# Another order for the last five chunks of an attention-and-adapters kernel

## The chip, the core and the metric

The kernel runs on one core of one Trainium2 chip, as one program. The metric is the device time of that program in microseconds. A core has TensorE (PE in the profile; PEld is its weight load), VectorE (DVE), ScalarE (ACT), GpSimd (POOL) and SyncE (SP), which here only issues DMAs. The engines run side by side; each takes its own instructions in order and waits where it needs what another has not finished.

## What is computed

Two stages follow each other. The first is attention with a pooled key and value: q is 4 x 12288 x 128, and kv, 4 x 384 x 32 x 128, is averaged over 4 x 4 patches into 768 keys of each batch.

```
kv_flat = kv_pool.reshape(B, -1, C) @ w_sr      # keys and values are the same rows
s = q @ kv_flat.T / sqrt(C);  a = softmax(s);  x = a @ kv_flat
```

The second is a mixture of eight small adapters on the 49152 rows x. The two largest of eight logits choose two adapters, and a softmax over those two gives their weights.

```
logits = x @ w_gate;  w = softmax(the two largest logits)
out = x + sum over the two of  w * ((x @ A[e]) @ B[e])      # A: 128x16, B: 16x128
```

## The kernel before, in words

The 49152 rows are handled as 96 **chunks** of 512 rows (T), each as 4 slices (S) of 128 rows, 24 chunks to a batch. K is the number of the last chunk, 95. For one chunk the steps are these, by the names of the code.

- `scores` makes the products of q and keys on TensorE in three rounds of 128x1024 into the PSUM tile sg, and ScalarE writes their exponentials into em (L246).
- `attend` multiplies em by the values extended with the gate's columns and a column of ones (vx); 24 matmuls accumulate into acc. Columns 0 to 127 are the unnormalised x, the next 8 the logits, the last the softmax's sum.
- `normalize` takes the reciprocal of the sums on VectorE (L258) and multiplies all 136 columns of the four slices (L263, 128x544) into xn.
- `top` sorts the eight logits of each slice with MAX8 (L281). `route` and `gates` make the two weights: four small operations on GpSimd (L293, L298, L299), a tanh on ScalarE (L312), and two more on GpSimd (L314, L315) into gw. A softmax over two is a tanh of half their difference. The tanh is put off in the list `later`.
- `transposes` and `down` turn x and multiply it by all eight A at once into h_ps. `gate` multiplies h_ps by gw into hg on VectorE (L347).
- hg is turned as well, `up` multiplies it by all eight B into d_ps, and `finish` adds d_ps and xn on VectorE (L360) and has SP store the 256 KB of the chunk (L361).

In the loop these steps of several chunks are woven into each other: while the scores of chunk k are made, chunk k-1 is attended and earlier ones pass the adapters. The order of every instruction on each engine is that of the program's text (`keep`): no scheduler moves any of it. When the loop ends, chunk K-5 is stored; K-4 has its hg turned and copied (tts) and still needs `up`, the addition and the store; K-3 has its hg, K-2 and K-1 wait with xn or acc, and K has only its exponentials. What follows is written out by hand with small helpers, and this **tail** is all that the change touches:

- `turn_x` and `turn_h` turn x or hg into a PSUM tile; `fetch` copies that into SBUF (tt) on ScalarE (L514, 128x512); `down_into` and `up_into` are the two adapter products; `gate_part` is the gate for some of the slices (L557).
- `part` is the attention of chunk K into the tile called o95.
- `add_here` adds and stores with VectorE reading PSUM (L542, then the DMA of L543). `carry` has ScalarE copy the product out of PSUM (L547), and `add_there` has GpSimd add xn to the copy and SP store it (L551, L552).
- `bank` gives PSUM: pool ps_m has two banks, ps_a one tile of two banks, ps_s two tiles of two banks. A tile that takes over a bank waits until its previous content has been read. Dependencies are kept for whole tiles: a write into one half of a tile waits for a reader of the other half.

In the tail before, chunk K is normalised in parts: VectorE makes the eight logit columns (L582, 128x32), ScalarE multiplies the 128 columns of x slice by slice (four instructions of 128x128, L585), and both begin when `part` is complete. Chunk K's weights are made on VectorE (L589 to L608) with a tanh on ScalarE (L606). K-4, K-1 and K (in halves) are added on VectorE, K-3 and K-2 go over ScalarE and GpSimd. K's hg is turned and copied in two halves (L634), K-1's in one piece. The last instruction with work is the addition of K's second half, and its store is the last one of the program.

Of the kernel before, what the change touches and what calls it, by code (L numbers as in the profile page):

```python
# [20 lines left out]
def kernel(  # L21
# [45 lines left out]
    def mm(*a, **k):  # L67
        return keep(nc.tensor.matmul(*a, **k))  # L68
# [187 lines left out]
    def normalize(k):  # L256
        ri = rpool.tile([P, S], FP32, tag="rinv", name="rinv")
        keep(nc.vector.reciprocal(ri, acc[k][:, :, VC]))  # L258
        k0, m = first[k], k - first[k]
        if m == 0:  # L260
            xg[k0] = xpool.tile([P, GC, S, VC], FP32, tag="xn", name="xn")
        x = xg[k0][:, m]
        keep(nc.vector.tensor_tensor(x, acc[k][:, :, 0:VC],  # L263
                                     ri.unsqueeze(2).broadcast_to([P, S, VC]), op=ALU.mult))
        xn[k] = x
# [19 lines left out]
    def route(k0):  # L285
        n = size[k0] * S
        eng = nc.gpsimd if k0 > 1 else nc.vector
        lg = xg[k0].rearrange("p m s c -> p (m s) c")[:, 0:n, C:VC]
        so = srt[k0].rearrange("p m s e -> p (m s) e")[:, 0:n]

        def over(i):
            d = rpool.tile([P, GC * S, 8], FP32, tag=f"over{i}", name=f"over{i}")[:, 0:n]
            keep(eng.tensor_tensor(  # L293
                d, lg, so[:, :, i].unsqueeze(2).broadcast_to([P, n, 8]), op=ALU.subtract))
            return d

        arg, mask = over(0), over(1)
        keep(eng.tensor_tensor(arg, arg, mask, op=ALU.add))  # L298
        keep(eng.tensor_scalar(mask, mask, 0.0, None, op0=ALU.is_ge))  # L299


        def rest():
            gates(k0, n, eng, arg, mask)

        if k0 > 3:
            later.append(rest)
        else:
            rest()
# [183 lines left out]
    def bank(pool):  # L492
        if pool is ps_m:
            return mtile([P, S, P], name="tail_ps")
        if pool is ps_a:
            return ps_a.tile([P, S, 256], FP32, tag="acc", name="acc")
        return ps_s.tile([P, 2, T], FP32, tag="sg", name="sg")

    def turn_x(k, pool):
        ps = bank(pool).bitcast(BF16).rearrange("p a b -> p (a b)")[:, 0:T].rearrange("p (s c) -> p s c", s=S)  # L500
        xb = xn[k].bitcast(U16)[:, :, 1::2].bitcast(BF16)
        for s in range(S):
            mm(ps[:, s], xb[:, s, 0:C], id_bf, is_transpose=True, start=(s == 0), stop=(s == S - 1))
        xT[k] = ps

    def turn_h(k, pool):
        ps = bank(pool).bitcast(BF16).rearrange("p a b -> p (a b)")[:, 0:T].rearrange("p (s c) -> p s c", s=S)
        for s in range(S):
            mm(ps[:, s], hg[k][:, s], id_bf, is_transpose=True, start=(s == 0), stop=(s == S - 1))
        hgT[k] = ps  # L510

    def fetch(which, k):
        sb = run.tile([P, S, P], BF16, tag="tt1", name="tt1")
        keep(nc.scalar.copy(sb, which[k]))  # L514
        which[k] = sb

    def part(k, o, js):
        for s in range(S):
            for j in js:
                mm(o[:, s, 0:VE], em[k][:, j, s * P:(s + 1) * P], vx[k // NB][:, j],  # L520
                   start=(j == 0 and s % 2 == 0), stop=(j == J - 1 and s % 2 == 1))

    def wide(o):
        return o.rearrange("p a b -> p (a b)")[:, 0:T].rearrange("p (s c) -> p s c", s=S)

    def down_into(k, pool):
        hp[k] = wide(bank(pool))
        for s in range(S):
            mm(hp[k][:, s], xT[k][:, s], a_bf, start=(s == 0), stop=(s == S - 1))

    def up_into(k, o):
        dp[k] = o
        for s in range(S):
            mm(o[:, s], hgT[k][:, s], b_bf, start=(s == 0), stop=(s == S - 1))
# [5 lines left out]
    def add_here(k, lo, hi, queue):  # L540
        osb = opool.tile([P, S, C], FP32, tag="osb", name="osb")[:, 0:hi - lo]
        keep(nc.vector.tensor_tensor(osb, dp[k][:, lo:hi], xn[k][:, lo:hi, 0:C], op=ALU.add))  # L542
        keep(queue.dma_start(dest(k)[:, lo:hi], osb))  # L543

    def carry(k):
        osb = opool.tile([P, S, C], FP32, tag="osb", name="osb")
        keep(nc.scalar.copy(osb, dp[k]))  # L547
        dp[k] = osb
# [5 lines left out]
    def gate_part(k, lo, hi):  # L554
        if lo == 0:
            hg[k] = run.tile([P, S, P], BF16, tag="hg", name="hg")
        keep(nc.vector.tensor_tensor(  # L557
            hg[k][:, lo:hi].rearrange("p s (e r) -> p (s e) r", e=E),
            hp[k][:, lo:hi].rearrange("p s (e r) -> p (s e) r", e=E),
            gw[k][:, lo:hi].rearrange("p s e -> p (s e)")  # L560
            .unsqueeze(2).broadcast_to([P, (hi - lo) * E, RK]), op=ALU.mult))

    turn_x(K - 2, ps_m)
    o95 = bank(ps_s).rearrange("p a (b c) -> p (a b) c", c=256)
    part(K, o95, range(4))
    turn_h(K - 3, ps_m)
    part(K, o95, range(4, J))
    fetch(xT, K - 2)
    for rest_ in later:
        rest_()  # L570
    later.clear()
    fetch(hgT, K - 3)

    normalize(K - 1)
    top(K - 1)
    route(K - 1)

    ri = rpool.tile([P, S], FP32, tag="rinv", name="rinv")
    keep(nc.vector.reciprocal(ri, o95[:, :, VC]))
    xn[K] = xpool.tile([P, GC, S, VC], FP32, tag="xn", name="xn")[:, 0]  # L580
    lg = rpool.tile([P, S, E], FP32, tag="lg", name="lg")
    keep(nc.vector.tensor_tensor(lg, o95[:, :, C:VC], ri.unsqueeze(2).broadcast_to([P, S, E]),  # L582
                                 op=ALU.mult))
    for s in range(S):
        keep(nc.scalar.activation(xn[K][:, s, 0:C], o95[:, s, 0:C], AF.Copy, bias=0.0,  # L585
                                  scale=ri[:, s:s + 1]))
    so = rpool.tile([P, S, 8], FP32, tag="so", name="so")
    for s in range(S):
        keep(nc.vector.max(so[:, s], lg[:, s]))  # L589
    mask = rpool.tile([P, S, E], FP32, tag="mk", name="mk")  # L590
    keep(nc.vector.tensor_tensor(mask, lg, so[:, :, 1].unsqueeze(2).broadcast_to([P, S, E]),
                                 op=ALU.is_ge))
    both = rpool.tile([P, S], FP32, tag="both", name="both")
    keep(nc.vector.tensor_tensor(both, so[:, :, 0], so[:, :, 1], op=ALU.add))
    keep(nc.vector.scalar_tensor_tensor(lg, lg, 2.0, both.unsqueeze(2).broadcast_to([P, S, E]),
                                        op0=ALU.mult, op1=ALU.subtract))

    down_into(K - 2, ps_m)
    gate_part(K - 2, 0, S)
    turn_x(K - 1, ps_m)  # L600
    dd = bank(ps_s)
    up_into(K - 4, wide(dd[:, 0:1]))
    up_into(K - 3, wide(dd[:, 1:2]))
    turn_x(K, ps_a)
    th = rpool.tile([P, S, E], FP32, tag="th1", name="th1")
    keep(nc.scalar.activation(th, lg, AF.Tanh, bias=0.0, scale=0.5))  # L606
    gw[K] = gpool.tile([P, S, E], FP32, tag="gw1", name="gw1")
    keep(nc.vector.scalar_tensor_tensor(gw[K], th, 1.0, mask, op0=ALU.add, op1=ALU.mult))  # L608
    fetch(xT, K - 1)
    fetch(xT, K)  # L610
    for rest_ in later:
        rest_()
    later.clear()
    carry(K - 3)
    add_there(K - 3)
    add_here(K - 4, 0, S, nc.sync)
    down_into(K - 1, ps_m)
    gate_part(K - 1, 0, S)
    turn_h(K - 2, ps_m)
    fetch(hgT, K - 2)  # L620
    down_into(K, ps_s)
    gate_part(K, 0, 2)
    gate_part(K, 2, S)
    up_into(K - 2, bank(ps_m))
    turn_h(K - 1, ps_a)
    fetch(hgT, K - 1)
    carry(K - 2)
    add_there(K - 2)
    ps = bank(ps_m).bitcast(BF16).rearrange("p a b -> p (a b)")[:, 0:T].rearrange("p (s c) -> p s c", s=S)
    hgT[K] = run.tile([P, S, P], BF16, tag="tt1", name="tt1")  # L630
    for lo in (0, 2):
        for s in range(lo, lo + 2):
            mm(ps[:, s], hg[K][:, s], id_bf, is_transpose=True, start=(s == lo), stop=(s == lo + 1))
        keep(nc.scalar.copy(hgT[K][:, lo:lo + 2], ps[:, lo:lo + 2]))  # L634
    up_into(K - 1, wide(bank(ps_s)))
    add_here(K - 1, 0, S, nc.sync)
    dp[K] = wide(bank(ps_s))
    for lo in (0, 2):
        for s in range(lo, lo + 2):
            mm(dp[K][:, s], hgT[K][:, s], b_bf, start=(s == lo), stop=(s == lo + 1))  # L640
        add_here(K, lo, lo + 2, nc.sync if lo else nc.scalar)


# [28 lines left out]
```

## Time and profile before

| what | value |
|---|---|
| time, median of 9 runs | 409.35 us (409.04 to 409.52) |
| the profiled execution | 409.23 us |
| its span in the profile | 407.2 us, so 2.0 us lie outside of it |
| busy: PE, DVE, ACT, POOL | 93%, 80%, 72%, 42% of the span |
| stretch 384 to 388 us (in the loop): PE busy | 3.95 of 4.00 us |
| stretch 396 to 398.5 us (in the tail): PE, DVE, ACT busy | 1.28, 1.19, 1.82 of 2.50 us |
| stretch 398.5 to 403.6 us: PE, DVE, ACT busy | 2.21, 2.27, 1.72 of 5.10 us |
| last addition (L542) ends | 403.56 us |

The profile comes from one execution, and times inside it count from its start. A line of the timeline gives start, duration (both us), engine, line, operation, the tile written and the tiles read, the shapes, and in brackets how long the engine had been idle and what ended that. A matmul's records overlap: four of 128x128 start some 0.056 us apart and each lasts 0.22 us, until its result is in PSUM. Instructions on ScalarE and VectorE overlap at their ends in the same way when the next one doesn't need the one before: copies of 128x512 on ScalarE last 0.6 us and start 0.47 us apart. "Granted clock" is the share of TensorE's full clock.

### The profile page before, as it was taken

To read this page: it belongs to the slowest core of one execution; us is meant where nothing else is said; L and a number is where in the kernel's file an instruction comes from. 1 tells how busy PE (TensorE), PEld (TensorE's weight loads), DVE (VectorE), ACT (ScalarE), POOL (GpSimd) and SP (SyncE) were. 2 spreads that over 40 slices of the span, in tenths; PEclk is the share of its full clock that TensorE was granted. 3 is DMA by queue.
4 is the path that set the end of the run, shared out by engine and by line. 5 is a ranking of instruction groups with operands and counts; after the bars stand their busy time and mean duration, and the time that the engine had idled before them with its cause. 6 is when DMAs were issued, how large, how long until landed. Compare 5 with 4: busy or idle time off the path is not lost.

```text
span 407.2 us, 11369 instructions
## 1 busy us (share of the span) xinstructions
PE 380.5 (93%) x4514; PEld 308.0 (76%) x4589; DVE 324.5 (80%) x948; ACT 292.9 (72%) x346; POOL 170.4 (42%) x289
## 2 busy tenths in 40 slices
PE   3898899999999999999999999999999999898992
PEld 3656678888888788888788878878888887777781
DVE  2543778988888888888988888888988888878873
ACT  2489468867678777867777877776777887666772
POOL 0010129778411319879311329879311322123342
PEclk9999999999999999999999999999999999999995
DMA  8997577974854999994745989996746548252213
GB/s 301 369 275 239 127 164 216 316 185 112 179 130 104 288 222 326 311 203 131 156 130 115 350 180 294 301 214 131 156 131 153 138 127 156 79 145 90 80 52 132
DMA packets 71319, 76.45 MB, mean 188 GB/s; under 512 B 49921, under 2 KB 50433, under 8 KB 70785
## 3 DMA queue, kind: packets, MB, share of 16 engines
q1 hardware_dynamic: 70128, 63.98, 53.3%
q0 software_dynamic: 704, 11.54, 16.2%
q8 instruction: 36, 0.59, 0.6%
q10 hardware_dynamic: 432, 0.20, 0.2%
q14 instruction: 19, 0.15, 0.1%
HBM read 50.53 MB, written 36.70 MB: 214 GB/s over the span
## 4 chain that ended last, share of the span: by engine, by line
PE 84%; DVE 7%; ACT 3%; issue 2%; DMA 1%; POOL 1%; ACTq 0%; DVEq 0%; POOLq 0%
PE acc L68 34%; PE sg L68 23%; PE tt_ps L68 10%; PE h_ps L68 6%; PE d_ps L68 5%; ACT em L246 2%; PE kpT_ps L68 2%; DVE rinv L258 1%; DVE xn L263 1%; DMA w_sr_sb<-in_w_sr_dram 1%; PE qT_ps L68 1%; DVE tts L333 1%; PE v_ps L68 1%; DVE hg L347 1%; PE kfT_ps L68 1%
## 5 line engine op out<-in xcount | busy, mean ns | idle before, releaser
L246 ACT ACTIVATE em<-sg 128x1024 f16<-128x1024 f32 x288 | 279.0, 1023 | 91.6 <-PE sg L68 60.1
L68 PE MATMUL acc<-vx,em 128*128 128x137 f16 x2280 | 171.7, 224 | 1.7 <-DVE xn L263 1.6
L68 PE MATMUL sg<-qT,kfT 128*128 128x512 bf16 x501 | 154.8, 379 | 2.7 <-ACT em L246 2.2
L68 PEld LDWEIGHTS <-em 128*128 128x128 f16 x2304 | 149.6, 98 | 4.0 <-DVE xn L263 2.2
L68 PEld LDWEIGHTS <-tts 128*128 128x128 bf16 x740 | 56.4, 98 | 45.8 <-DVE tts L333 2.1
L293 POOL TENSOR_TENSOR over<-xn,srt 128x128 f32<-128x128 f32 (+2 forms) x62 | 21.4, 363 | 156.9 <-DVE srt L281 156.9
L347 DVE TENSOR_TENSOR hg<-h_ps,gw 128x512 bf16<-128x512 f32 x93 | 64.2, 690 | 13.1 <-POOL gw L315 7.6
L263 DVE TENSOR_TENSOR xn<-acc,rinv 128x544 f32<-128x544 f32 x95 | 68.8, 724 | 3.3
L333 DVE COPY tts<-tt_ps 128x1024 bf16<-128x1024 bf16 (+1 forms) x96 | 64.4, 671 | 3.6 <-PE tt_ps L68 3.6
L171 POOL TENSOR_TENSOR kvr<-kvr 128x512 f32<-128x512 f32 x54 | 66.7, 1272 | 0.0
L360 DVE TENSOR_TENSOR osb<-d_ps,xn 128x512 f32<-128x512 f32 x91 | 62.6, 690 | 0.5 <-PE d_ps L68 0.5
L68 PEld LDWEIGHTS <-kfT 128*128 128x128 bf16 x576 | 45.9, 97 | 6.0 <-issue 3.7
L68 PEld LDWEIGHTS <-xn 128*128 128x128 bf16 x384 | 29.4, 98 | 22.0 <-ACT xn L585 0.5
L258 DVE RECIPROCAL rinv<-acc 128x4 f32<-128x4 f32 x95 | 17.2, 182 | 32.6 <-PE acc L68 31.4
L68 PE MATMUL h_ps<-a_bf,tts 128*128 128x128 bf16 x372 | 36.0, 219 | 2.8 <-DVE tts L333 1.6
L68 PE MATMUL tt_ps<-id_bf,xn 128*128 128x128 bf16 x372 | 36.0, 219 | 1.5
L68 PE MATMUL d_ps<-b_bf,tts 128*128 128x128 bf16 x364 | 35.2, 219 | 2.3 <-DVE tts L333 1.3
L68 PE MATMUL tt_ps<-id_bf,hg 128*128 128x128 bf16 x368 | 35.6, 219 | 0.3 <-DVE hg L347 0.3
L281 DVE MAX8 srt<-xn 128x8 f32<-128x8 f32 x380 | 34.3, 153 | 0.2
L314 POOL TENSOR_TENSOR gw<-th,over 128x128 f32<-128x128 f32 (+2 forms) x31 | 12.0, 388 | 39.3 <-ACT th L312 39.2
L68 PEld LDWEIGHTS <-hg 128*128 128x128 bf16 x384 | 25.7, 98 | 2.5 <-issue 1.3
L169 POOL TENSOR_TENSOR kvr<-kvr 128x512 f32<-128x512 f32 (+1 forms) x18 | 18.1, 1006 | 0.9
(77 smaller groups left out, 176.7 us busy)
## 6 DMA issues: line engine op xcount, KB each, us to landing
out_dram<-osb SPq DMA_DIRECT2D x95, 256.0 KB, 3.4
kvr<-in_kv_dram SPq DMA_DIRECT2D x36, 512.0 KB, 6.1
qbf<-in_q_dram POOLq DMA_DIRECT2D x22, 512.0 KB, 6.5
kvr<-in_kv_dram SPq DMA_DIRECT2D x24, 256.0 KB, 5.0
qf<-in_q_dram SPq DMA_DIRECT2D x1, 1024.0 KB, 5.1
qf<-in_q_dram SPq DMA_DIRECT2D x4, 256.0 KB, 5.3
qT<-qbf SPq DMA_TRANSPOSE x22, 6.3
out_dram<-osb ACTq DMA_DIRECT2D x1, 128.0 KB, 3.1
```

The source lines that it names most:

```text
L68: return keep(nc.tensor.matmul(*a, **k))
L169: keep(adder.tensor_tensor(u, u, v, op=ALU.add))
L171: keep(adder.tensor_tensor(u[:, lo:hi], u[:, lo:hi], v[:, lo:hi], op=ALU.add))
L246: keep(nc.scalar.activation(em[k][:, 2 * r:2 * r + 2], ps, AF.Exp, bias=0.0, scale=scale))
L258: keep(nc.vector.reciprocal(ri, acc[k][:, :, VC]))
L263: keep(nc.vector.tensor_tensor(x, acc[k][:, :, 0:VC], ri.unsqueeze(2).broadcast_to([P, S, VC]), op=ALU.mult))
L281: keep(nc.vector.max(srt[k0][:, m, s], xn[k][:, s, C:VC]))
L293: keep(eng.tensor_tensor(d, lg, so[:, :, i].unsqueeze(2).broadcast_to([P, n, 8]), op=ALU.subtract))
L314: keep(eng.tensor_tensor(w[:, 0:n], th, mask, op=ALU.mult))
L333: keep(nc.vector.tensor_copy(sb[:, lo:hi], ps[:, lo:hi]))
L347: keep(nc.vector.tensor_tensor(hg[k].rearrange("p s (e r) -> p (s e) r", e=E), hp[k].rearrange("p s (e r) -> p (s e) r", e=E), gw[k0][:, m ...
L360: keep(nc.vector.tensor_tensor(osb, dp[k], xn[k][:, :, 0:C], op=ALU.add))
```

## The change

Only the tail is written anew; what it computes stays. In the new order:

- `up_into(K-4)` stands ahead of the first part of K's attention, and K-4 goes over ScalarE and GpSimd (`carry`, `add_there`) where VectorE added it before. K-2 is added on VectorE in its place: K-4 and K-3 pass GpSimd's adder, where K-3 and K-2 did.
- K-2 passes `down_into` and its gate, and K-1 is turned, ahead of the second part of K's attention. The turning of K-3's hg follows it.
- Chunk K is normalised by the `normalize` of the loop, as one 128x544 instruction on VectorE; the four ScalarE multiplications and the small one for the logits are gone. K's weights come from the logit columns of xn, with the mask made after the tanh's argument.
- K-1's gate stands after K's, and both are cut into halves. The turning, the copy out and the product with B of K and K-1 are cut into halves as well, in the order K first half, K second half, K-1 first half, K-1 second half. The additions come in the order K-2, K (two), K-1 (two), and K-1's second half is stored last.

```diff
@@ -514,6 +514,11 @@
         keep(nc.scalar.copy(sb, which[k]))
         which[k] = sb
 
+    def tanhs():
+        for rest_ in later:
+            rest_()
+        later.clear()
+
     def part(k, o, js):
         for s in range(S):
             for j in js:
@@ -561,84 +566,84 @@
             .unsqueeze(2).broadcast_to([P, (hi - lo) * E, RK]), op=ALU.mult))
 
     turn_x(K - 2, ps_m)
+    up_into(K - 4, bank(ps_m))
     o95 = bank(ps_s).rearrange("p a (b c) -> p (a b) c", c=256)
     part(K, o95, range(4))
-    turn_h(K - 3, ps_m)
+    fetch(xT, K - 2)
+    tanhs()
+    down_into(K - 2, ps_m)
+    carry(K - 4)
+    normalize(K - 1)
+    turn_x(K - 1, ps_m)
     part(K, o95, range(4, J))
-    fetch(xT, K - 2)
-    for rest_ in later:
-        rest_()
-    later.clear()
-    fetch(hgT, K - 3)
-
-    normalize(K - 1)
+    turn_h(K - 3, ps_a)
+    fetch(xT, K - 1)
     top(K - 1)
     route(K - 1)
-
-    ri = rpool.tile([P, S], FP32, tag="rinv", name="rinv")
-    keep(nc.vector.reciprocal(ri, o95[:, :, VC]))
-    xn[K] = xpool.tile([P, GC, S, VC], FP32, tag="xn", name="xn")[:, 0]
-    lg = rpool.tile([P, S, E], FP32, tag="lg", name="lg")
-    keep(nc.vector.tensor_tensor(lg, o95[:, :, C:VC], ri.unsqueeze(2).broadcast_to([P, S, E]),
-                                 op=ALU.mult))
-    for s in range(S):
-        keep(nc.scalar.activation(xn[K][:, s, 0:C], o95[:, s, 0:C], AF.Copy, bias=0.0,
-                                  scale=ri[:, s:s + 1]))
+    gate_part(K - 2, 0, S)
+    add_there(K - 4)
+
+    acc[K] = o95
+    normalize(K)
+    lg = xn[K][:, :, C:VC]
+    tanhs()
     so = rpool.tile([P, S, 8], FP32, tag="so", name="so")
     for s in range(S):
         keep(nc.vector.max(so[:, s], lg[:, s]))
     mask = rpool.tile([P, S, E], FP32, tag="mk", name="mk")
+    both = rpool.tile([P, S], FP32, tag="both", name="both")
+    keep(nc.vector.tensor_tensor(both, so[:, :, 0], so[:, :, 1], op=ALU.add))
+    arg = rpool.tile([P, S, E], FP32, tag="arg1", name="arg1")
+    keep(nc.vector.scalar_tensor_tensor(arg, lg, 2.0, both.unsqueeze(2).broadcast_to([P, S, E]),
+                                        op0=ALU.mult, op1=ALU.subtract))
     keep(nc.vector.tensor_tensor(mask, lg, so[:, :, 1].unsqueeze(2).broadcast_to([P, S, E]),
                                  op=ALU.is_ge))
-    both = rpool.tile([P, S], FP32, tag="both", name="both")
-    keep(nc.vector.tensor_tensor(both, so[:, :, 0], so[:, :, 1], op=ALU.add))
-    keep(nc.vector.scalar_tensor_tensor(lg, lg, 2.0, both.unsqueeze(2).broadcast_to([P, S, E]),
-                                        op0=ALU.mult, op1=ALU.subtract))
-
-    down_into(K - 2, ps_m)
-    gate_part(K - 2, 0, S)
-    turn_x(K - 1, ps_m)
-    dd = bank(ps_s)
-    up_into(K - 4, wide(dd[:, 0:1]))
-    up_into(K - 3, wide(dd[:, 1:2]))
-    turn_x(K, ps_a)
+
+    down_into(K - 1, ps_m)
+    turn_h(K - 2, ps_s)
+    turn_x(K, ps_m)
+    fetch(hgT, K - 3)
+    up_into(K - 3, wide(bank(ps_a)))
+    fetch(xT, K)
     th = rpool.tile([P, S, E], FP32, tag="th1", name="th1")
-    keep(nc.scalar.activation(th, lg, AF.Tanh, bias=0.0, scale=0.5))
+    keep(nc.scalar.activation(th, arg, AF.Tanh, bias=0.0, scale=0.5))
     gw[K] = gpool.tile([P, S, E], FP32, tag="gw1", name="gw1")
     keep(nc.vector.scalar_tensor_tensor(gw[K], th, 1.0, mask, op0=ALU.add, op1=ALU.mult))
-    fetch(xT, K - 1)
-    fetch(xT, K)
-    for rest_ in later:
-        rest_()
-    later.clear()
+    down_into(K, ps_s)
+    fetch(hgT, K - 2)
     carry(K - 3)
     add_there(K - 3)
-    add_here(K - 4, 0, S, nc.sync)
-    down_into(K - 1, ps_m)
-    gate_part(K - 1, 0, S)
-    turn_h(K - 2, ps_m)
-    fetch(hgT, K - 2)
-    down_into(K, ps_s)
-    gate_part(K, 0, 2)
-    gate_part(K, 2, S)
-    up_into(K - 2, bank(ps_m))
-    turn_h(K - 1, ps_a)
-    fetch(hgT, K - 1)
-    carry(K - 2)
-    add_there(K - 2)
-    ps = bank(ps_m).bitcast(BF16).rearrange("p a b -> p (a b)")[:, 0:T].rearrange("p (s c) -> p s c", s=S)
-    hgT[K] = run.tile([P, S, P], BF16, tag="tt1", name="tt1")
-    for lo in (0, 2):
+    halves = [(K, 0), (K, 2), (K - 1, 0), (K - 1, 2)]
+    for k, lo in halves:
+        gate_part(k, lo, lo + 2)
+    up_into(K - 2, wide(bank(ps_s)))
+    dp[K] = wide(bank(ps_a))
+    turned = {k: bank(ps_m).bitcast(BF16).rearrange("p a b -> p (a b)")[:, 0:T]
+              .rearrange("p (s c) -> p s c", s=S) for k in (K - 1, K)}
+    for k in turned:
+        hgT[k] = run.tile([P, S, P], BF16, tag="tt1", name="tt1")
+
+    def half(ks, lo, lhs, rhs, transpose):
         for s in range(lo, lo + 2):
-            mm(ps[:, s], hg[K][:, s], id_bf, is_transpose=True, start=(s == lo), stop=(s == lo + 1))
-        keep(nc.scalar.copy(hgT[K][:, lo:lo + 2], ps[:, lo:lo + 2]))
-    up_into(K - 1, wide(bank(ps_s)))
-    add_here(K - 1, 0, S, nc.sync)
-    dp[K] = wide(bank(ps_s))
-    for lo in (0, 2):
-        for s in range(lo, lo + 2):
-            mm(dp[K][:, s], hgT[K][:, s], b_bf, start=(s == lo), stop=(s == lo + 1))
-        add_here(K, lo, lo + 2, nc.sync if lo else nc.scalar)
+            kw = dict(is_transpose=True) if transpose else {}
+            mm(ks[:, s], lhs[:, s], rhs, start=(s == lo), stop=(s == lo + 1), **kw)
+
+    for k, lo in halves:
+        half(turned[k], lo, hg[k], id_bf, True)
+        keep(nc.scalar.copy(hgT[k][:, lo:lo + 2], turned[k][:, lo:lo + 2]))
+        if (k, lo) == (K, 2):
+            half(dp[K], 0, hgT[K], b_bf, False)
+            add_here(K - 2, 0, S, nc.sync)
+        elif k < K:
+            if lo == 0:
+                half(dp[K], 2, hgT[K], b_bf, False)
+                add_here(K, 0, 2, nc.sync)
+                add_here(K, 2, S, nc.sync)
+    dp[K - 1] = bank(ps_m)
+    half(dp[K - 1], 0, hgT[K - 1], b_bf, False)
+    add_here(K - 1, 0, 2, nc.scalar)
+    half(dp[K - 1], 2, hgT[K - 1], b_bf, False)
+    add_here(K - 1, 2, S, nc.sync)
 
 
 # ---- launch: one core; inputs and outputs as the reference has them ----
```

## The prediction, made before the changed kernel ran

> **What bounds the kernel now.** I read three views: the page's slices, the chain of work that ended last, and the timeline of the tail. In the loop TensorE is busy 3.95 of 4 us, and nothing ahead of 391.9 us changes (the two programs have the same instructions there), so only the tail can move. The first fence is from the chain, cut to the tail: start, duration, what was worked on.
>
> ```profile
> 392.27 0.99 PE sg L68 x16
> ...
> 394.51 1.14 ACT xn L585 x4
> ...
> 397.97 0.69 DVE hg L557
> ...
> 400.48 0.29 ACT tt L634
> ...
> 402.73 0.39 PE sg L68 x2
> 403.11 0.02 issue
> 403.14 0.42 DVE osb L542
> ```
>
> From 394 us no engine is full: the chain passes from TensorE to ScalarE to VectorE and back, a relay. What counts is when each hand-over happens. The timeline has the rows that I price by:
>
> ```profile
> 393.17 0.25 POOL L314 TENSOR_TENSOR gw<-th,over 128x32 f32<-128x32 f32 x1 [1.03 <-ACT th L312]
> 393.50 0.25 POOL L315 TENSOR_TENSOR gw<-gw,over 128x32 f32<-128x32 f32 x1
> 394.02 0.18 DVE L579 RECIPROCAL rinv<-sg 128x4 f32<-128x4 f32 x1 [0.58 <-PE sg L68]
> ...
> 396.71 0.62 ACT L547 COPY osb<-sg 128x512 f32<-128x512 f32 x1
> 397.37 0.69 DVE L542 TENSOR_TENSOR osb<-sg,xn 128x512 f32<-128x512 f32 x1 [1.31 <-ACT osb L547]
> 397.54 1.26 POOL L551 TENSOR_TENSOR osb<-osb,xn 128x512 f32<-128x512 f32 x1
> 398.57 0.75 DVE L557 TENSOR_TENSOR hg<-sg,gw 128x256 bf16<-128x256 f32 x2
> 400.37 0.39 ACT L634 COPY tt<-tail_ps 128x256 bf16<-128x256 bf16 x1
> 402.37 1.55 SPq L543 DMA_DIRECT2D out_dram<-osb  x2
> ```
>
> K's gate (the x2 at 398.57) stands on VectorE behind K-4's addition, which sat idle 1.31 us until ScalarE's copy had ended, and behind K-1's gate. K-1's own copies then hold K's halves up again (400.37), and the last store is issued at 403.59 (402.37 + 1.55, less its 0.33). The third fence, table by stage, has the granted clock after the five engines:
>
> ```profile
> 397.00:398.50 1.50, 0.58 (x8) 0.23 (x5) 1.13 (x2) 0.82 (x2) 1.42 (x3) 1.00 0.04 11
> 398.50:400.00 1.50, 0.82 (x6) 0.66 (x7) 0.82 (x3) 0.59 (x2) 0.30 (x1) 0.50 0.22 83
> ```
>
> TensorE falls to half clock at 398.5. The last 128 KB store then lands 2.5 us after its issue by the DMA view (406.09), and 1.1 us later the span ends.
>
> **Unit prices, all from the tail's rows.** Four 128x128 matmuls give their result 0.39 us after they start and hold TensorE 0.22; two take 0.28, at half clock 0.37 to 0.42. Hand-overs: TensorE to VectorE 0.04, VectorE or ScalarE to TensorE 0.05, TensorE to ScalarE 0.04 to 0.09. ScalarE: 512 columns 0.60 (the next starts 0.47 after), 256 columns 0.39, tanh 0.24 (the next 0.13 after). VectorE: gate or addition 0.69, a half 0.42 (the next 0.33 after).
>
> **Up to K's attention.** `up_into(K-4)` adds four matmuls ahead of the first part: it starts at 392.33 where it was 392.11, and TensorE goes on at 393.33. ScalarE copies K-2's turned x as before (392.31 to 392.89), the tanh follows, then the moved `carry(K-4)`, 392.92 to 393.54. Its DMA waits are for stores of chunks up to K-10, long landed. Queued behind it on TensorE, K-1's turning wants the carry's bank: `down_into(K-2)` fills 393.33 to 393.55, so it starts at 393.59, 0.04 late. Then the second part, eight at 0.062: result at 394.47. It was 393.98: **0.49 us lost** here. K-2's gate waits for gw (393.75, as now) and runs 393.80 to 394.50, so the reciprocal isn't held: 394.53 to 394.71.
>
> **Chunk K.** One 128x544 instruction (0.72, row of L263) replaces the small one and four ScalarE ones (1.14): xn is complete at 395.48, not 395.65. Turning 395.53 to 395.92; copy at once, 396.01 to 396.62, where K-1's copy was ahead of it; `down_into(K)` done at 397.06 (was 397.18). Beside it VectorE makes the weights: MAX8 0.37, sum 0.16, argument 0.19 with gaps of 0.03 end at 396.30; the tanh starts 0.47 behind the copy, 396.48; gw at 396.98. K's gate starts at **397.10 instead of 398.57**: 1.47 us gained, since neither K-4's addition nor K-1's gate is in front.
>
> What hides the rest: K-2's second copy (to 397.2) and its product end at 397.7, VectorE needs it at 398.43. On GpSimd `add_there(K-4)` stands ahead of K-1's weights: 394.94 to 396.20, then two of 0.25, gw at 396.9, needed at 397.77: 0.9 us of cover. Past that each delay goes straight to K-1's halves. K-3's carry runs 397.1 to 397.7, ahead of the first half copy (397.94); GpSimd adds until 399.06. SP has K-3's store (399.09) ahead of K-2's, whose addition ends at 399.12: no wait.
>
> **The halves.** K: gates 397.10 and 397.43 to 397.85; K-1: 397.77 and 398.10 to 398.51. K first half turned 397.57 to 397.85, copied 397.94 to 398.33. The second half writes the same tile, so it waits for that copy: 398.38 to 398.66, copied to 399.09. K-1's first half, behind K's first product, at half clock: 398.70 to 399.10, copied to 399.54. K's second product 399.14 to 399.56; both additions wait for it: 399.60 and 399.93 to 400.35. K-1's second half waits for its first copy: 399.59 to 400.01, copied to 400.44; K-1's first product, to 400.22, is added to 400.68. The second product is in the tile that this addition reads: 400.73 to 401.10, added 401.14 to 401.56. Last store at **401.59, against 403.59: 2.00 us less**, 1.47 from the gate and 0.53 behind it (4.49 us from gate to store against 5.02).
>
> **The stores.** K-4's goes out at 396.2 and lands some 3 us later, before the last addition takes over its buffer. K-3, K-2 and four halves, 1.05 MB, are issued from 399.09 on. The DMA view shows 337 to 437 GB/s while it moves, and data some 0.9 us after an issue: 2.6 us at 400 GB/s end at 402.6. The last store by itself moves its 0.33 us from 402.5, so the queue is just free: 2.5 us to landing stand, with 0.3 to 0.5 more at the slowest slices' rate.
>
> Sum: 409.23 (profiled) - 2.0 = 407.2. The median of the runs is 0.12 above the profiled one: **407.4**. The bound below which this kernel can't tell a change is 0.2%, 0.82 us.
>
> **A rule against the change.** In the trace of before, VectorE's small operations on chunk K (L591 to L608) ran while GpSimd was idle (394.86 to 397.01), and the gates that ran beside GpSimd's 1.26 us addition took 0.68 as otherwise; they read one operand from PSUM. The Trainium skill, "SBUF — State Buffer", Who interferes with whom, says that a VectorE instruction with two SBUF inputs and a GpSimd one that reads SBUF hold each other off for a whole instruction. In the new order the sum, argument and mask fall beside GpSimd's addition and K-1's weights. By the rule the sum would start at 396.2 instead of 395.92, and I estimate K's gate 0.1 to 0.35 later, 407.5 to 407.7; by the rows 407.4. No row shows the case.
>
> **Unknown costs.** VectorE beside GpSimd: between nothing (the gate's row) and 1.26 an addition (L551); the gate's row is nearest, I take nothing, and a gain is excluded, as no row has an instruction shorter for a neighbour. Half clock: the drop may fall elsewhere. If it came at 395, two groups of four (0.25 each) and two pairs (0.14) of the chain are slower, +0.8; if not before the end, three pairs faster, -0.4. I take 398.5. The rest of the ordering has no price beyond those.
>
> **Rivals.**
> 1. Part of it is given back: the clock drops early (+0.8) or the stores queue (+0.3 to 0.5). For: stretches from 395 have TensorE busy only 0.58 of 1.5 us; six stores in 2.5 us. Against: the clock held to 398.5 in before with hardly more matmuls. Some 408.2.
> 2. No change: a whole-tile wait or GpSimd's queue takes the place of VectorE's. If gw of K-1 came 2.9 us later than my sum, K-1's halves would end where K's did. For: it is made behind an addition that waits for ScalarE. Against: 0.9 us of cover, and ScalarE loses 1.14 us of work. 409.3.
> 3. Slower: GpSimd's two additions hold VectorE for their whole length, once over K's normalising and MAX8, once over K-1's gates and K-2's addition: 2 x 1.26 = 2.5 on the chain. It decides from 2.0 on: 409.9. For: both now lie where VectorE is the relay's runner. Against: 0.68 for the gate beside 1.26 in the trace of before.
>
> **How the numbers follow.** Forecast, 406.9 to 408.0: 0.66; better (clock held), below 406.9: 0.06; rival 1: 0.17, about two thirds of it still beyond 0.2%; rival 2: 0.06; rival 3 and slower: 0.05. Faster 0.66 + 0.06 + 0.12 = 0.84, same 0.11, slower 0.05. The range takes in the held clock (407.0, less the spread of 0.4) and most of rival 1 (+0.8 and some): 406.6 to 408.6.
>
> **What would show it.** In the profile after: carry of K-4 ending about 393.5 and o95 complete near 394.5; L263 for K at 394.7; K's first gate near 397.1; K-1's second addition ending near 401.6; the last store landing 2.5 us after. Wrong if K's gate starts after 398, if a VectorE instruction stands beside L556 longer than its row here, if half clock shows from 395, or if the last store lands more than 3 us after its issue.

## The result, and the profile after

The changed kernel takes 407.07 us (median of 9 runs, 406.75 to 407.66) against 409.28 us (29 runs) for the kernel before: ratio 0.9950, 95% interval 0.9942 to 0.9958, so 2.2 us less. Forecast was 407.4, range 406.6 to 408.6. The profiled execution took 407.36 us with a span of 405.5.

In this execution the tail begins 0.26 us later than in the one before (first matmul that turns K-2's x: 392.15 against 391.89), with nothing changed ahead of it. To compare, I count **tail time** from that matmul. First the chain that ended last, cut to the tail (start, duration, work):

```profile
392.76 0.99 PE sg L68 x16
...
394.94 0.73 DVE xn L263
...
396.83 0.58 ACT tt L514
...
398.88 0.38 ACT tt L633
...
400.77 0.39 PE tail_ps L68 x2
401.16 0.02 issue
401.18 0.42 DVE osb L547
```

It is still a relay, but K-4's addition and K-1's gate are gone from it: it comes from K's normalising (L263) through two copies (L514) to the copies of halves (L633). The timeline's rows that answer to those of before:

```profile
393.19 0.58 ACT L552 COPY osb<-tail_ps 128x512 f32<-128x512 f32 x1
...
394.94 0.72 DVE L263 TENSOR_TENSOR xn<-sg,rinv 128x544 f32<-128x544 f32 x1
...
395.09 1.27 POOL L556 TENSOR_TENSOR osb<-osb,xn 128x512 f32<-128x512 f32 x1
...
396.11 0.27 DVE L595 TENSOR_TENSOR both<-so 128x4 f32<-128x4 f32 x1
...
397.29 0.76 DVE L562 TENSOR_TENSOR hg<-sg,gw 128x256 bf16<-128x256 f32 x2
...
399.69 2.36 SPq L548 DMA_DIRECT2D out_dram<-osb  x4
```

K's gate starts at 397.29 (tail time 5.14; 6.68 before). The last store is issued at 401.63, tail time 9.48 against 11.70. One row is longer than its like in before, where the sum was L594:

```profile
394.98 0.16 DVE L594 TENSOR_TENSOR both<-so 128x4 f32<-128x4 f32 x1
```

L595 takes 0.27 us where that took 0.16, and it ends at 396.38, just after GpSimd's addition (395.09 + 1.27 = 396.36). By stage (granted clock, DMA share and GB/s are the last three columns):

```profile
398.50:400.00 1.50, 1.16 (x12) 0.70 (x11) 1.18 (x4) 0.78 (x4) 0.73 (x1) 1.00 0.03 12
400.00:402.00 2.00, 0.37 (x2) 0.20 (x2) 1.14 (x4) 0.26 (x1) 0.00 (x0) 0.60 0.98 364
```

Two things differ from what I had summed: the clock holds until 400.39, and the DMA engines, which I had as just free for the last store, are full from 400 on (0.98) and still move 213 GB/s from 402.65 to 403.15, while TensorE has two matmuls left.

### The profile page after: what moved, and what is told of

It reads as the page before. It is cut to its first block, busy times and chain, and to the rows that moved or that the text cites. A ratio compares the mean times of both kernels' runs of the same rounds, so it can differ in the third digit from the quotient of the medians.

```text
span 405.5 us, 11373 instructions
## 1 busy us (share of the span) xinstructions
PE 378.9 (93%) x4514; PEld 306.5 (76%) x4589; DVE 325.4 (80%) x950; ACT 292.2 (72%) x343; POOL 170.4 (42%) x289
## 4 chain that ended last, share of the span: by engine, by line
PE 82%; DVE 7%; ACT 3%; DMA 3%; issue 2%; SPq 1%; POOL 1%; ACTq 0%; DVEq 0%; POOLq 0%
PE acc L68 34%; PE sg L68 23%; PE tt_ps L68 10%; PE h_ps L68 6%; PE d_ps L68 5%; ACT em L246 2%; DVE xn L263 2%; DVE rinv L258 1%; DMA w_sr_sb<-in_w_sr_dram 1%; SPq L98 1%; PE kpT_ps L68 1%; DMA kvr<-in_kv_dram 1%; DVE tts L333 1%; PE v_ps L68 1%; DVE hg L347 1%
## 5 line engine op out<-in xcount | busy, mean ns | idle before, releaser
L263 DVE TENSOR_TENSOR xn<-acc,rinv 128x544 f32<-128x544 f32 x95 | 68.8, 725 | 3.3
```

The lines of the kernel that those rows point to most:

```text
L263: keep(nc.vector.tensor_tensor(x, acc[k][:, :, 0:VC], ri.unsqueeze(2).broadcast_to([P, S, VC]), op=ALU.mult))
```

## The experiments

All on one core. "Gate" is the start of K's gate, "issued" the start of the last store's issue, "landed" the last completion of a store in the trace, all in tail time; ratios are to the kernel before, measured beside it.

| run | gate | issued | landed | median us | ratio (95%) |
|---|---|---|---|---|---|
| before | 6.68 | 11.70 | 14.19 | 409.28 | 1 |
| after | 5.14 | 9.48 | 12.20 | 407.07 | 0.9950 (0.9942 to 0.9958) |
| e1, after again | 5.14 | 9.44 | 12.11 | 407.65 | 0.9959 (0.9946 to 0.9971) |
| e12, after again | 5.14 | 9.48 | 12.02 | 407.16 | 0.9952 (0.9940 to 0.9965) |
| e2 | 6.34 | 11.14 | 13.64 | 408.94 | 0.9993 (0.9985 to 1.0002) |
| e3 | 5.33 | 11.61 | 13.55 | 408.71 | 0.9985 (0.9976 to 0.9993) |
| e9 | 5.34 | 10.57 | 12.88 | 408.0 | 0.9973 (0.9963 to 0.9983) |
| e4 | 5.59 | 9.91 | 11.97 | 406.99 | 0.9947 (0.9934 to 0.9961) |
| e5 | 5.14 | 8.56 | 12.19 | 407.17 | 0.9948 (0.9936 to 0.9961) |
| e6 | 5.14 | 9.02 | 12.17 | 407.45 | 0.9954 (0.9941 to 0.9968) |
| e7 | 5.79 | 10.46 | 12.63 | 407.61 | 0.9959 (0.9944 to 0.9974) |
| e8, one time | 5.70 | 10.10 | 12.68 | 407.91 | - |
| e10 | 5.14 | 8.58 | 11.69 | 406.98 | 0.9945 (0.9932 to 0.9957) |
| e11 | 5.14 | 8.59 | 11.64 | 406.76 | 0.9942 (0.9929 to 0.9956) |

**e1 and e12: the changed kernel again.**

> The changed kernel unaltered, as the base for the others of this call. In its first profile K's gate started 397.29, the last store was issued at 401.63 and half clock began at 400.39, where the kernel before had half clock from 398.50. If the gain is one of order (theory), this run is 2.0 to 2.4 us faster again, whenever the clock drops; the distances between the tail's instructions stay within 0.1 us. If the gain came from the clock that happened to hold 1.9 us longer (rival), a profile in which the clock drops as early as in the kernel before has its last store 0.4 us or more later behind K's gate, and the gain is below 1.7 us.

> The changed kernel unaltered, as the base of this call: ratio to the kernel before 0.994 to 0.996, its last store issued 9.4 to 9.5 us after the tail's start and landed near 12.1.

The start of K's gate and the last issue keep their places within 0.05 us. Half clock began at tail time 8.24, 8.70 and 7.99 in the three profiles, and the gain is 1.6 to 2.2 us; the 1.6 of e1 is less than the 2.0 expected. The rival's own test, a drop in this kernel as early as in before (6.61), did not occur. Two other profiles bear on it: in e2, which keeps most of the old order, the drop came at 7.95, as late as in e12 (7.99), and its last store landed at 13.64 against 12.02; in e7, the changed kernel but for one part, it came at 6.28, and the last store landed at 12.63 against 14.19 in before. So most of the gain doesn't come from the clock; how much of the rest does, no run says.

**e2 and e3: VectorE's order alone, in the kernel before.** e2 moves K-4's addition behind K's gates, e3 K's gates also ahead of K-1's.

```diff
-    add_here(K - 4, 0, S, nc.sync)
     down_into(K - 1, ps_m)
-    gate_part(K - 1, 0, S)                   # e3 only
...
     gate_part(K, 2, S)
+    gate_part(K - 1, 0, S)                   # e3 only
+    add_here(K - 4, 0, S, nc.sync)
```

> Kernel before, with K-4's addition moved behind K's gates on VectorE, and nothing else. The prediction gave 1.47 us of gain to K's gate no longer standing behind K-4's addition and K-1's gate. If the addition is what holds it, K's gate moves forward by its 0.60 us and the time falls by about 0.6 us. If K-1's gate waits for its weights anyway (made on GpSimd by 397.59 in before, since their tanh stands behind copies on ScalarE), the forward move is only 0.3 us (397.67 for K-1's gate instead of 397.97), and the time falls by 0.3.

> Kernel before, with K's gates ahead of both K-1's gate and K-4's addition on VectorE: the new order of VectorE alone, with the old order of TensorE and ScalarE. K's gate should start near 397.2, as in the changed kernel. If that start is what sets the end (the prediction's 1.47 us), the time falls by 1.2 to 1.5 us. If the end is set by the relay behind it, in which K-1's turning, copy and carry stand ahead of K's halves on TensorE and ScalarE, K's halves wait for K-1's gate as before (398.6) and the time falls by less than 0.3 us.

e2: the gate moves 0.34 us, as the second reading says, for K-1's gate waits for its weights anyway. The time can't be told from no change. e3 is the telling one: the gate starts at 5.33, near its place in the changed kernel (5.14), and the last store is issued only 0.09 us earlier. VectorE's gates (K's two halves, then K-1's) and ScalarE's copies in e3 show where it goes:

```profile
397.66 0.76 DVE L557 TENSOR_TENSOR hg<-sg,gw 128x256 bf16<-128x256 f32 x2 [1.16 <-PE sg L68]
398.33 0.68 DVE L557 TENSOR_TENSOR hg<-tail_ps,gw 128x512 bf16<-128x512 f32 x1
...
399.77 0.58 ACT L514 COPY tt<-acc 128x512 bf16<-128x512 bf16 x1 [1.51 <-PE acc L68]
400.25 0.59 ACT L547 COPY osb<-tail_ps 128x512 f32<-128x512 f32 x1
400.73 0.39 ACT L634 COPY tt<-tail_ps 128x256 bf16<-128x256 bf16 x1
```

K's first half (L634) waits behind K-1's copy and K-2's carry, and ScalarE is idle for 1.51 us until K-1's hg, gated from 398.33 on (tail time 6.00; 6.09 in before), is turned. So K's first half is copied at tail time 8.40 where it was 8.48 in before: it follows K-1's gate, not its own. The time fell by 0.5 us all the same; in the profile that is the landing, 1.94 us after the issue instead of 2.49, with stores of the same sizes in front. Why it landed sooner stays open; it is not the gate's 1.35 us.

**e9: the order of TensorE and ScalarE behind the gates, in the kernel of e3.**

```diff
-    turn_h(K - 1, ps_a)
-    fetch(hgT, K - 1)
-    carry(K - 2)
-    add_there(K - 2)
...                                           # K's hg is turned in ps_a, not ps_m
-    up_into(K - 1, wide(bank(ps_s)))
-    add_here(K - 1, 0, S, nc.sync)
     dp[K] = wide(bank(ps_s))
     for lo in (0, 2):
         for s in range(lo, lo + 2):
             mm(dp[K][:, s], hgT[K][:, s], b_bf, start=(s == lo), stop=(s == lo + 1))
-        add_here(K, lo, lo + 2, nc.sync if lo else nc.scalar)
+        if lo == 0:
+            turn_h(K - 1, ps_m)
+    fetch(hgT, K - 1)
+    carry(K - 2)
+    add_here(K, 0, 2, nc.sync)
+    add_here(K, 2, S, nc.sync)
+    up_into(K - 1, wide(bank(ps_s)))
+    add_here(K - 1, 0, S, nc.sync)
+    add_there(K - 2)
```

> The kernel of e3 (before, with K's gates first on VectorE) with the order behind the gates changed too: on TensorE and ScalarE both halves of K's turned hg and their copies stand ahead of K-1's turning and copy and of K-2's carry, K's additions ahead of K-1's, K-2 stored last. All else is as in the kernel before: K normalised on two engines, K-4 added on VectorE, K-3 and K-2 on GpSimd, K-1 in one piece. By e3's rows the last store is issued near 9.6 us after the tail's start instead of 11.6, with 1.28 MB from 6.95 on. If the gain of the change is the order of the relay behind K's gate, this gives 1.6 to 2.2 us against the kernel before. If it is K's single normalising, the other way of K-4 or the halves of K-1, it gives less than 0.8.

1.2 us by the medians, 1.13 us at the last issue: between my two figures, and the last store is issued at 10.57, not near 9.6. About half of the gain comes with this order and e3's together. To e3 alone the order behind the gates adds 1.04 us at the last issue, and some 0.5 us of time by the ratios; the order without the early gate was not run. What ends e9 is K-2, whose way over ScalarE and GpSimd is the last to be done:

```profile
398.76 0.37 ACT L630 COPY tt<-acc 128x256 bf16<-128x256 bf16 x1 [0.66 <-PE acc L68]
399.60 0.37 ACT L630 COPY tt<-acc 128x256 bf16<-128x256 bf16 x1 [0.46 <-PE acc L68]
...
401.44 1.26 POOL L551 TENSOR_TENSOR osb<-osb,xn 128x512 f32<-128x512 f32 x1 [2.34 <-ACT osb L547]
```

K's halves (the first two rows) are now copied without waiting for K-1. The changed kernel gates K-2 at tail time 1.93 instead of 3.40 and adds it on VectorE. That step, with the rest of the change, is the other 1.1 us at the last issue (10.57 to 9.48); half clock, which began at 6.97 in e9's profile and at 8.24 in that of the changed kernel, may have a part in it. No run separates these.

**e4 and e5: the relay made longer and shorter in the changed kernel.** e4 puts K-1's half gates ahead of K's; e5 gives every half a PSUM tile of its own and lets ScalarE issue two stores.

```diff
-    for k, lo in halves:                             # e4
+    for k, lo in halves[2:] + halves[:2]:
         gate_part(k, lo, lo + 2)
...
-        half(turned[k], lo, hg[k], id_bf, True)      # e5
+    turn_half(K, 0, ps_m)
+    turn_half(K, 2, ps_s)
...
+    dp[K - 1] = wide(bank(ps_s))
+    up_half(K - 1, 0)
...
+    dp[K - 1] = wide(bank(ps_s))
+    up_half(K - 1, 2)
```

> Changed kernel, with K-1's two half gates ahead of K's on VectorE, the order of the others kept. K's gate then starts 0.5 to 0.66 us later. If K's gate is on the chain through both chunks' halves, the last store and the time are 0.5 to 0.7 us later than in the changed kernel. If the end hangs on K-1's halves, whose gate is now earlier, the time is the same within 0.2 us.

> Changed kernel with its relay behind the gates shortened: each half of K's and K-1's turned hg, and each half of K-1's product, gets a PSUM tile of its own, so that no half waits for the reader of the other, and two stores are issued by ScalarE. The last store should be issued 0.7 to 0.95 us earlier, near 400.7. If the relay sets the end, as the prediction's sum has it, the time falls by 0.7 to 0.9 us against the changed kernel. If the stream of the six stores sets it (1.05 MB from K-3's store on, DMA engines full), the last store only waits longer to land, and the time falls by less than 0.3 us.

Last issue at 9.91 (e4), 9.48 (after) and 8.56 (e5), last landing at 11.97, 12.20 and 12.19: 1.35 us of relay make no difference to the end. (The last issue does follow K's gate: in e4 the gate is 0.45 us later and the issue 0.43.) The stage 400 to 402 us of e5:

```profile
400.00:402.00 2.00, 0.00 (x0) 0.00 (x0) 0.61 (x2) 0.00 (x0) 0.00 (x0) 0.99 0.99 363
```

TensorE, ScalarE and GpSimd are done, the DMA engines are full. In e4 the last store lands 2.06 us after its issue, in e5 it needs 3.63: in e5 it waits for the stores in front, in e4 hardly. The issue of K-3's store is what the three have in common, at tail time 7.11 or 7.12, and with it begins a stream of six stores (1.05 MB). The reading is that in the changed kernel this stream sets the end; e10 tests it.

**e10 and e11: that stream begun earlier.** e10 is e5 with K-3's carry ahead of K-2's copy (and K-2's product behind K's first turning, left out below); e11 is e10 with GpSimd's addition of K-3 and its store in two halves.

```diff
-    fetch(hgT, K - 2)
     carry(K - 3)
     add_there(K - 3)
+    fetch(hgT, K - 2)
```

> The kernel of e5 with K-3's carry ahead of the copy of K-2's turned hg on ScalarE (and K-2's product behind K's first turning on TensorE), so that GpSimd adds K-3 and SP stores it some 0.5 us earlier (6.6 instead of 7.1 us after the tail's start). If the end is set by the stream of stores that begins with K-3's, the last landing and the time are 0.4 to 0.5 us earlier than in e5, though the last store is issued no earlier. If something else sets it (a fixed landing time of the last store), the time is that of e5.

> The kernel of e10 with K-3's addition on GpSimd and its store in two halves: the first 128 KB go out another 0.6 us earlier, near 6.0 us after the tail's start. If the stream sets the end, another 0.3 to 0.6 us less than e10, until the last store's own landing (issued near 8.6, 2.0 us to land without a queue) takes over. Otherwise no change from e10.

K-3's store, in the changed kernel and in e10:

```profile
399.26 0.33 SPq L557 DMA_DIRECT2D out_dram<-osb  x1
```

```profile
398.76 0.33 SPq L557 DMA_DIRECT2D out_dram<-osb  x1
```

e10: first store 0.45 us earlier than in e5 (6.67), last issue unchanged, last landing 0.50 us earlier. That is the stream theory's answer in the profile; the time is not shown to follow (ratio 0.9945 against 0.9948, where 0.4 to 0.5 us would be 0.001, and the intervals are as wide). The other profiles agree: in all nine whose last stores are K-3's, K-2's, K's and K-1's, 1.05 MB in that order (after, e1, e12, e4 to e8, e10), the last landing comes 4.85 to 5.09 us after K-3's store is issued, while the last issue lies 1.44 to 2.80 us after it. In e4 and e7 the last store lands 2.06 and 2.17 us after its own issue, so there its issue sets the end as much. e11 begins at 6.14 and ends only 0.05 us sooner: its DMA rate shows gaps (238 and 303 GB/s in the two half microseconds from 399.7, where e10 has 393 and 397), since K-3's second half is issued only 0.68 us after the first. By the timed runs e10 and e11 are 0.2 and 0.4 us below e12, inside the intervals: not measurably better than the changed kernel.

**e6 and e7: two parts of the change undone.** e6 handles K-1 in one piece (one gate, copy, product, addition and store); e7 normalises K as before, logits on VectorE and x in four instructions on ScalarE.

> Changed kernel with K-1 again in one piece (gate, turning, copy, product, addition, one store of 256 KB), K still in halves. By the rows the addition of K-1 would run 400.30 to 401.0, so its store is issued 0.6 us earlier than the changed kernel's last one, with twice the bytes. If halving K-1 brought part of the 0.53 us, as the prediction has it, this is 0.2 us or more slower. If the stream of stores sets the end, it is the same within 0.2 us; if the relay does, 0.3 us faster.

> Changed kernel with chunk K normalised as before: VectorE the logit columns, ScalarE the other 128 in four instructions. Those hold ScalarE 1.14 us in front of the copy of K's turned x, so K's gate should start 0.4 us later (theory: the one 128x544 instruction is the better one). If the end hangs on K's gate, the time rises by 0.4 us; if on the stores, by less than 0.2. Rival for the part: the logits come 0.5 us earlier and K's gate starts no later than in the changed kernel.

e6: issued 0.46 us earlier, landed the same. Halving K-1 brings nothing here. e7: K's gate 0.65 us later, landed 0.43 later in the profile, the ratio's interval overlaps that of the changed kernel. K's gate is late because the four instructions hold ScalarE until 396.37: the copy of K's turned x starts at 396.83 instead of 396.21, and the tanh stands behind it. K-3's store is late too (7.77), so the stream begins 0.66 later. The logits' earlier start is lost besides: the sum (0.80 us here) waits for GpSimd's addition.

**e8: GpSimd's addition moved over K's weights.**

```diff
-    add_there(K - 4)                         # ahead of normalize(K)
+    add_there(K - 4)                         # behind the weights of K-1
```

> Changed kernel with GpSimd's addition of K-4 moved behind the weights of K-1, so that it runs some 0.8 us later, over the sum, argument, mask and weights of chunk K on VectorE, all of which read two SBUF tiles. In the changed kernel the sum took 0.27 us instead of 0.16 and ended 0.02 us after that addition. If the two engines hold each other off, the sum ends when the addition does, 0.6 to 0.7 us later than in the changed kernel, and K's gate starts that much later. If the 0.27 was something else, the sum takes 0.16 us and K's gate starts where it did or 0.1 us earlier.

GpSimd's row, then VectorE's:

```profile
395.82 1.26 POOL L556 TENSOR_TENSOR osb<-osb,xn 128x512 f32<-128x512 f32 x1
```

```profile
396.18 0.92 DVE L595 TENSOR_TENSOR both<-so 128x4 f32<-128x4 f32 x1
397.13 0.19 DVE L597 SCALAR_TENSOR_TENSOR arg<-xn,both 128x32 f32<-128x32 f32 x1
```

An instruction of 128x4 lasts 0.92 us and ends at 397.10, 0.02 after the addition (397.08). VectorE's sum does wait until GpSimd's addition ends, and K's gate is 0.56 us later. In all ten profiles in which the two overlap the sum ends 0.02 us after the addition. The addition itself is not longer for it (1.26 us as in before).

## Why the prediction was right, and where it was wrong

**The places of the tail** came out as summed. Set back by the 0.26 us of the later start: the reciprocal 394.47 (394.53 predicted), xn complete 395.41 (395.48), K's gate 397.03 (397.10), last issue 401.37 (401.59). The loss on TensorE (o95 complete 2.55 us into the tail, 2.10 in before: 0.45, priced 0.49) and the hidden carry of K-4 are as priced too.

**"1.47 us gained" at the gate failed as a cause.** The gate moved as said, but e3 moves it almost as far alone, and the last issue comes 0.09 us earlier. I read the chain's most visible idle time as the bound and did not follow what stood behind it on ScalarE. In the new order the last issue follows the gate (e4), but the early gate alone is not enough: with the order of the copies and products behind it, it makes 1.13 us of the 2.22 at the last issue (e9). How the other 1.09 divide among K-2's earlier way and the rest of the change is not shown. The 0.53 us behind the gate measured 0.68 (11.70 - 6.68 = 5.02, 9.48 - 5.14 = 4.34).

**"The queue is just free" failed.** The last store lands 2.72 us after its issue, and e4, e5 and e6 show that its issue may move by 1.35 us without moving the end. The working gave the stream's end as 402.6, with "0.3 to 0.5 more at the slowest slices' rate" kept for the range; by the profiles it was the bound. (The DMA view from which I took 337 to 437 GB/s also has a slice of 164 in the same stretch.) Two errors were of opposite sign: the store stream cost 0.2 us more than I took, the relay 0.2 less. That the last landing moved by just the 2.0 us of the sum (14.19 to 12.20) is in part luck.

**Half clock** came at 400.39, not 398.5. Only the last pair of matmuls ran slow (0.37 for 0.27). K's second product took 0.29 us where the sum has 0.42, which is most of the relay's 0.2 us.

**The rule weighed against the change held.** The sum L595 waited for GpSimd's addition, 0.11 us in the changed kernel and 0.76 in e8, as the Trainium skill has it ("SBUF — State Buffer", Who interferes with whom). I took nothing by the gate's row, which has only one SBUF input and did not show the case; one of the signs of being wrong that I named, a VectorE instruction longer beside L556 than alone, did come. For GpSimd's small instructions the rows can't tell: the argument L597 (396.42, 0.20 us, 0.19 alone) ends 0.05 us after GpSimd's 128x32 instruction (396.32 to 396.57), as it would with a wait or without.

**Rivals.** Of the first, the queue of stores is real: 0.2 us more to landing than summed, 0.7 more than the 2.06 of e4. The early drop of the clock did not come; the "0.58 of 1.5 us" cited for it is the stretch from 397 to 398.5 alone, and from 395 to 397 TensorE was busy 1.56 of 2.00 us. The second and third did not come: beside GpSimd's additions only the sum, with two SBUF inputs, was longer, by 0.11 us and not 2.5; K's normalising (0.72) and K-1's gates (0.74 for two halves) took what they take alone.

## What to carry to other kernels

Before crediting a gain to a step that moves earlier, follow its result through the in-order queues behind it: in e3 the early gate waited in ScalarE's queue as long as before. At the end of a kernel, lay the last stores out as a stream, from its first issue, its bytes and the measured rate; when that stream ends later than the last addition plus one landing, move the first store earlier (0.45 us there moved the last landing by 0.50, in e10's profile), not the last (0.92 us there moved it by 0.01, in e5's). On VectorE, keep instructions with two SBUF inputs off the time of long GpSimd instructions (0.92 us instead of 0.16 in e8).

## What was not expected of the hardware

Landing varied with stores of the same sizes in front: 1.94 us from issue in e3, 2.49 in before. SP needed 0.33 to 0.41 us to issue a store in the changed kernel, so that K's second half was issued 0.28 us after its addition had ended (400.66 against 400.39). And half clock began between tail time 6.2 and 10.6 in these profiles, in the changed kernel alone between 8.0 and 8.7.
